# A Fourier-mixing and GEGLU kernel: even slots, and a channel stage of one pass per parity fed by sums and differences

## The chip, the cores and the metric

The kernel runs on one core of a Trainium2 chip. The metric is the device time of one execution in microseconds (us). Each run also has a profile of one execution, whose span is some 2 us shorter than the timed runs. A ratio is the mean time of one kernel's runs over the mean of the other kernel's runs of the same rounds, so it is not quite the ratio of the medians that are quoted.

## The reference, cut to what matters

```python
def _attn_ref(x):                      # x: 8 x 3008 x 256
    X = np.fft.fft(x, axis=1)
    X = np.fft.fft(X, axis=2)
    return X.real.astype(np.float32)

def _moe_ref(x, w_gate, w_val, w_out): # 24064 x 256, 256 x 1536 twice, 1536 x 256
    g = x @ w_gate
    gelu = 0.5 * g * (1.0 + erf(g * inv_sqrt2))
    return (gelu * (x @ w_val) @ w_out).astype(np.float32)
```

## The kernel before

Each batch (8 of them) goes through a Fourier part (the DFT, a discrete Fourier transform) of three stages and then through the two layers. The DFT of batch b+1 is woven as "filler" into the layers of batch b. In the profiles TensorE's results stand in tiles in PSUM (named `ps_...`), and ACT or DVE copy them ("evict" them) to tiles in SBUF (named `..._sb`, `A` and `Z` among them). A read "in steps of 192 bytes" is one whose consecutive elements lie 192 bytes apart. What matters here:

- Stage 1 multiplies x by a factor matrix `G`, four values of j at a time, for channels 0 to 127 and for 128 to 255. Each half is copied from PSUM to `A`.
- The channel stage multiplies `A` by cosines and sines `CS`: two passes of 256 columns for each k2, which add up the two halves of the channels in PSUM. The result goes to `Z`.
- A batch is 36 slots: three chunks of tokens times 12 slices (`fc`) of the 1536 hidden units. A slot holds the first layer of one slice (gate and value), some second-layer matmuls of the chunk before, and perhaps a piece of filler.
- The head is the DFT of batch 0, which has no layers to hide behind.

```python
        def s1_ev(j0, engines):
            for cc in range(2):
                src = _sub(st.pop((j0, cc)), [[1, 2 * K2H], [96, 4], [2 * K2H, 2]], 0)
                dst = _sub(st["A"], [[64, 2 * K2H], [2, 4], [1, 2]], cc * K2H * 128 + j0 * 2)
                if engines[cc] == "A":
                    nc.scalar.activation(dst, src, AF.Copy)
                else:
                    nc.vector.tensor_copy(dst, src)
# ... (cut)
        def ch_pack(k2):
            # ... (cut)
                for d in range(2):
                    for cc in range(2):
                        nc.tensor.matmul(ps[:, d * C : (d + 1) * C], A[:, cc, k2 + d, :], CS[:, cc, :],
                                         start=(cc == 0), stop=(cc == 1))
                if b == 0 and k2 // 2 % 2 == 1:
                    nc.scalar.activation(_sub(Z, [[1, 2 * C]], k2 * C), ps, AF.Copy)
                else:
                    nc.vector.tensor_copy(_sub(Z, [[1, 2 * C]], k2 * C), ps)
# ... (cut: the loop over slots)
            for fc in range(NFC):
                first[fc]()                      # gate E, O -> gelu; value -> DVE
                # ... filler pieces up to this slot's share ...
                if fc > 0:
                    second[fc - 1]()             # gate M -> gelu, value M -> h
                tgt = len(pend) * (fc + 1) // NFC
                while done < tgt:                # second layer: units of 12 matmuls,
                    pend[done]()                 # so none or one in a slot
                    done += 1
```

## Time and profile before

| | before |
|---|---|
| time, median of 3 | 719.55 us (718.97 to 719.59) |
| TensorE (PE) busy | 96% of the span |
| VectorE (DVE), ScalarE (ACT), GpSimd (POOL) busy | 80%, 65%, 58% |
| first channel matmul | at 20.5 us |
| one batch in steady state | 84.9 us |

The page of the kernel before: the span, the busy time of each engine (share of the span, instructions), and the chain of work that ended last, by engine.

```profile
span 716.7 us, 14298 instructions
## 1 busy us (share of the span) xinstructions
PE 688.0 (96%) x5274; PEld 460.5 (64%) x5336; DVE 572.3 (80%) x923; ACT 466.9 (65%) x892; POOL 412.2 (58%) x242
...
PE 88%; ACT 5%; DVE 4%; issue 2%; DMA 1%; POOL 0%; ACTq 0%; DVEq 0%
```

PE leads in both views. A busy PE is not yet a full one, because records of matmuls overlap. So I also added up, from the records, the distances between starts of matmuls, less the median distance for each shape. What remains is PE's waits. A record that is missing from the trace looks like a wait of exactly one matmul's length; those gaps were left out. Between 60 us and the last 20 us this gives 19.5 us of waits, mostly in pieces of 0.1 to 0.3 us. How close to a matmul's length a gap must be to be left out is a choice: with others this sum lies between 15 and 20 us. Another 16 us lie in the first 40 us.

Groups of instructions by line, with shapes kept apart, of the kernel before. After `xcount` come the busy time in us, the mean of one in ns, and the engine's idle time just before them.

```profile
L402 PE MATMUL ps_dft<-CS,A_sb 128*128 128x256 bf16 x372 | 60.8, 274 | 0.4 <-DVE EO_sb L456 0.3
L412 DVE CAST Z_sb<-ps_dft 128x512 bf16<-128x512 f32 x88 | 60.1, 684 | 1.3 <-PE ps_dft L402 1.3
L379 ACT ACTIVATE A_sb<-ps_dft 128x384 bf16<-128x384 f32 x115 | 50.9, 496 | 0.3 <-PE ps_dft L365 0.3
```

In the head DVE also made six of these copies of stage 1. The view of tile `A_sb` of the kernel before shows the duration of two of them as minimum, median and maximum (the other four took 558 ns too); this is the number from which the cost of the new adds was estimated.

```profile
L381 DVE CAST A_sb<-ps_dft x2: 558/558/558, 15.6 to 19.9; 128x384 bf16<-128x384 f32 x2
```

Busy time by stretch, of one steady batch of the kernel before. The first row is the stage-1 stretch (from the first stage-1 matmul of the next batch to its first channel matmul), the second the channel stretch (from there to the next batch's stage 1). The columns are the length, then busy us and count of PE, weight loads, DVE, ACT and POOL, then clock, DMA share and GB/s.

```profile
199.50:224.20 24.70, 24.45 (x202) 16.64 (x204) 19.09 (x31) 18.82 (x40) 15.37 (x8) 1.00 0.24 47
224.20:284.40 60.20, 59.79 (x458) 40.26 (x462) 50.36 (x82) 37.67 (x70) 36.18 (x19) 1.00 0.27 59
```

PE is busy for nearly all of both. DVE has 5.6 us free in the stage-1 stretch (24.7 less 19.1).

### The profile page before, as it was taken

To read this page: it belongs to the slowest core of one execution; us is meant where nothing else is said; L and a number is where in the kernel's file an instruction comes from. 1 tells how busy PE (TensorE), PEld (TensorE's weight loads), DVE (VectorE), ACT (ScalarE), POOL (GpSimd) and SP (SyncE) were. 2 spreads that over 40 slices of the span, in tenths; PEclk is the share of its full clock that TensorE was granted. 3 is DMA by queue.
4 is the path that set the end of the run, shared out by engine and by line. 5 is a ranking of instruction groups with operands and counts; after the bars stand their busy time and mean duration, and the time that the engine had idled before them with its cause. 6 is when DMAs were issued, how large, how long until landed. Compare 5 with 4: busy or idle time off the path is not lost.

```text
span 716.7 us, 14298 instructions
## 1 busy us (share of the span) xinstructions
PE 688.0 (96%) x5274; PEld 460.5 (64%) x5336; DVE 572.3 (80%) x923; ACT 466.9 (65%) x892; POOL 412.2 (58%) x242
## 2 busy tenths in 40 slices
PE   2899999999999999999999999999999999999995
PEld 2556666666667666666666666666666766666664
DVE  7698888798877888788877888779887788888870
ACT  6688567766676666766677656776668666666650
POOL 8205565655556565666566656555565656576760
PEclk9999999999999999999999999999999999999999
DMA  9951512431115111151212421111111111211122
GB/s 247 205 118 23 124 31 46 86 72 35 41 38 119 42 34 43 33 121 38 45 31 53 105 45 34 43 36 37 35 41 42 30 44 31 45 41 38 42 45 66
DMA packets 36277, 43.43 MB, mean 61 GB/s; under 512 B 6668, under 2 KB 33292, under 8 KB 34700
## 3 DMA queue, kind: packets, MB, share of 16 engines
q1 hardware_dynamic: 32432, 30.47, 17.8%
q0 software_dynamic: 3184, 11.57, 8.8%
q8 instruction: 41, 0.67, 0.4%
q10 hardware_dynamic: 592, 0.49, 0.3%
q14 instruction: 28, 0.23, 0.1%
HBM read 29.43 MB, written 24.64 MB: 75 GB/s over the span
## 4 chain that ended last, share of the span: by engine, by line
PE 88%; ACT 5%; DVE 4%; issue 2%; DMA 1%; POOL 0%; ACTq 0%; DVEq 0%
PE ps_o L573 33%; PE ps_g L502 23%; PE ps_v L502 20%; PE ps_dft L402 6%; PE ps_dft L365 3%; ACT gelu_sb L517 1%; ACT gelu_sb L554 1%; ACT A_sb L379 1%; PE ps_dft L427 1%; PE ps_dft L440 1%; DVE x_sb L236 1%; ACT out_sb L591 1%; DVE EO_sb L456 1%; PE ps_dft L452 1%; DVE h_sb L536 1%
## 5 line engine op out<-in xcount | busy, mean ns | idle before, releaser
L551 POOL TENSOR_TENSOR h_sb<-gelu_sb,v_sb 128x1024 bf16<-128x1024 bf16 (+1 forms) x184 | 387.1, 2105 | 277.2 <-ACT gelu_sb L550 156.8
L573 PE MATMUL ps_o<-Wo_sb,h_sb 128*128 128x256 bf16 (+1 forms) x2304 | 295.5, 272 | 4.0 <-DVE out_sb L584 2.2
L573 PEld LDWEIGHTS <-h_sb 128*128 128x128 bf16 (+1 forms) x2304 | 227.7, 100 | 68.3 <-issue 9.4
L517 ACT ACTIVATE gelu_sb<-ps_g 128x512 bf16<-128x512 f32 (+1 forms) x288 | 169.8, 590 | 123.2 <-PE ps_g L502 115.2
L524 DVE SCALAR_TENSOR_TENSOR ve_sb<-EB_sb,w_97,ps_v 128x512 f32<-128x512 bf16 (+1 forms) x184 | 134.1, 733 | 66.2 <-PE ps_v L502 66.0
L528 DVE SCALAR_TENSOR_TENSOR v_sb<-ps_v,ve_sb 128x512 f32<-128x512 f32 (+1 forms) x184 | 124.4, 676 | 13.9 <-POOL h_sb L551 0.5
L530 DVE SCALAR_TENSOR_TENSOR v_sb<-ps_v,ve_sb 128x512 f32<-128x512 f32 (+1 forms) x184 | 123.3, 670 | 0.0
L550 ACT ACTIVATE gelu_sb<-ps_g 128x512 bf16<-128x512 f32 (+1 forms) x184 | 108.6, 590 | 19.2 <-PE ps_g L502 17.7
L502 PE MATMUL ps_v<-EO_sb,WvE 128*128 128x512 bf16 (+1 forms) x288 | 107.8, 374 | 3.2
L502 PE MATMUL ps_g<-EO_sb,WgE 128*128 128x512 bf16 (+1 forms) x287 | 107.4, 374 | 1.6
L502 PE MATMUL ps_v<-EO_sb,WvM 128*128 128x512 bf16 (+1 forms) x288 | 108.0, 375 | 0.3 <-DVE v_sb L530 0.2
L502 PE MATMUL ps_g<-EO_sb,WgM 128*128 128x512 bf16 (+1 forms) x287 | 107.9, 376 | 0.1
L555 DVE TENSOR_TENSOR h_sb<-gelu_sb,ps_v 128x512 bf16<-128x512 bf16 (+1 forms) x104 | 69.7, 671 | 32.5 <-ACT gelu_sb L554 32.5
L591 ACT ACTIVATE out_sb<-ps_o 128x512 f32<-128x512 f32 x92 | 54.8, 595 | 51.2 <-PE ps_o L573 51.2
L502 PE MATMUL ps_g<-EO_sb,WgO 128*128 128x512 bf16 (+1 forms) x231 | 86.4, 374 | 0.0
L536 DVE TENSOR_TENSOR h_sb<-gelu_sb,ps_v 128x512 bf16<-128x512 bf16 (+1 forms) x104 | 69.9, 673 | 5.2 <-ACT gelu_sb L517 4.0
L554 ACT ACTIVATE gelu_sb<-ps_g 128x512 bf16<-128x512 f32 (+1 forms) x104 | 61.0, 590 | 6.3 <-PE ps_g L502 6.2
L412 DVE CAST Z_sb<-ps_dft 128x512 bf16<-128x512 f32 x88 | 60.1, 684 | 1.3 <-PE ps_dft L402 1.3
L402 PE MATMUL ps_dft<-CS,A_sb 128*128 128x256 bf16 x372 | 60.8, 274 | 0.4 <-DVE EO_sb L456 0.3
L402 PEld LDWEIGHTS <-A_sb 128*128 128x128 bf16 x384 | 37.8, 99 | 28.9 <-issue 1.8
L365 PEld LDWEIGHTS <-x_sb 94*128 94x128 bf16 x512 | 31.9, 102 | 31.3 <-DVE x_sb L236 14.9
L379 ACT ACTIVATE A_sb<-ps_dft 128x384 bf16<-128x384 f32 x115 | 50.9, 496 | 0.3 <-PE ps_dft L365 0.3
(102 smaller groups left out, 433.2 us busy)
## 6 DMA issues: line engine op xcount, KB each, us to landing
out_dram<-out_sb SPq DMA_DIRECT2D x361, 64.0 KB, 2.0
x_sb<-in_x_dram POOLq DMA_DIRECT2D x14, 752.0 KB, 8.1
x_plain<-in_x_dram SPq DMA_DIRECT2D x4, 384.0 KB, 7.6
x_plain<-in_x_dram SPq DMA_DIRECT2D x2, 768.0 KB, 7.6
Wo_sb<-in_moe_w_out_dram POOLq DMA_DIRECT2D x2, 384.0 KB, 5.8
wg_hi<-in_moe_w_gate_dram SPq DMA_DIRECT2D x2, 256.0 KB, 3.8
wv_hi<-in_moe_w_val_dram SPq DMA_DIRECT2D x2, 256.0 KB
wg_lo<-in_moe_w_gate_dram SPq DMA_DIRECT2D x2, 256.0 KB, 4.4
```

The source lines that it names most:

```text
L402: nc.tensor.matmul(ps[:, d * C : (d + 1) * C], A[:, cc, k2 + d, :], CS[:, cc, :], start=(cc == 0), stop=(cc == 1),)
L502: nc.tensor.matmul(ps[:, :n], W[nm, part][:, fs], src, start=start, stop=stop, **kw)
L517: nc.scalar.activation(gl[:, 0, :n], pg[:, :n], AF.Gelu)
L524: nc.vector.scalar_tensor_tensor(ve[:, :n], EB_bufs[b][:, c0 : c0 + n], w128[:, fc : fc + 1], pv[:, :n], op0=ALU.mult, op1=ALU.add)
L528: nc.vector.scalar_tensor_tensor(vv[:, 0, :n], po[:, :n], -0.5, ve[:, :n], op0=ALU.mult, op1=ALU.add)
L530: nc.vector.scalar_tensor_tensor(_sub(vv, [[-1, n]], TOK + n - 1), po[:, :n], 0.5, ve[:, :n], op0=ALU.mult, op1=ALU.add)
L536: nc.vector.tensor_tensor(st["h"][:, fc, 0, :n], gl[:, 0, :n], pv[:, :n], op=ALU.mult)
L550: nc.scalar.activation(_sub(gl, [[-1, n]], TOK + n - 1), pg[:, :n], AF.Gelu)
L551: nc.gpsimd.tensor_tensor(st["h"][:, fc, :, :n], gl[:, :, :n], pv[:, :, :n], op=ALU.mult)
L554: nc.scalar.activation(gl[:, 1, :n], pg[:, :n], AF.Gelu)
L555: nc.vector.tensor_tensor(_sub(st["h"], [[-1, n]], (fc * 2 + 1) * TOK + n - 1), gl[:, 1, :n], pv[:, :n], op=ALU.mult)
L573: nc.tensor.matmul(pso[:m, sign, :], st["h"][:, fc, sign, h0 : h0 + m], Wo_sb[:, fc, :], start=(fc == 0), stop=(fc == NFC - 1),)
```

## The change

Two changes come together.

1. **One channel pass per parity.** With sums s = a(c) + a(c+128) and differences d = a(c) - a(c+128), the even output channels need s alone and the odd ones d alone. Each is one pass of 128 columns in place of two of 256, which halves the columns that the channel stage streams. The sums and differences are made as stage 1 leaves PSUM: ACT copies the upper half to SBUF (`up`, fp32), and DVE adds and subtracts. To make room on DVE, `Z` is copied by ACT.
2. **Even slots.** The second layer is cut into pieces of four matmuls, two in every slot. The second gate pass of a slice comes directly after the first gate pass of the next slice.

```diff
-        def s1_ev(j0, engines):
-            for cc in range(2):
-                src = _sub(st.pop((j0, cc)), [[1, 2 * K2H], [96, 4], [2 * K2H, 2]], 0)
-                dst = ...
-                ACT or DVE copy
+        def s1_ev(j0):
+            up = up_tile()                                  # 128 x 384, fp32, 2 buffers
+            nc.scalar.activation(up, st.pop((j0, 1))[:, 0:384], AF.Copy)
+            lo, hi = (_sub(t, [[1, 2 * K2H], [96, 4], [2 * K2H, 2]], 0) for t in (st.pop((j0, 0)), up))
+            for g, op in enumerate((ALU.add, ALU.subtract)):
+                dst = _sub(st["A"], [[64, 2 * K2H], [2, 4], [1, 2]], g * K2H * 128 + j0 * 2)
+                nc.vector.tensor_tensor(dst, lo, hi, op=op)
 ...
                 for d in range(2):
-                    for cc in range(2):
-                        nc.tensor.matmul(ps[:, d * C : (d + 1) * C], A[:, cc, k2 + d, :], CS[:, cc, :],
-                                         start=(cc == 0), stop=(cc == 1))
+                    for g in range(2):
+                        o = g * C + d * 128
+                        nc.tensor.matmul(ps[:, o : o + 128], A[:, g, k2 + d, :], CS[:, g, :], start=True, stop=True)
+                dst = _sub(Z, [[1, 2 * C]], k2 * C)
+                src = _sub(ps, [[64, 4], [1, 64], [C, 2]], 0)
                 if b == 0 and k2 // 2 % 2 == 1:
-                    nc.scalar.activation(...)
+                    nc.vector.tensor_copy(dst, src)
                 else:
-                    nc.vector.tensor_copy(...)
+                    nc.scalar.activation(dst, src, AF.Copy)
 ... (cut: CS is 2 x 128 columns; output buffers 3 -> 2; layer functions split in four: G, V, g, v)
+        L2P = 4                                             # second layer: pieces of four matmuls
+    SLOT = "GgVvfLL"   # gate, second gate of the slice before, value, second value, filler, two pieces
 ...
+            for fc in range(NFC + 1):
+                for step in SLOT:
+                    if step in "GV" and fc < NFC:
+                        parts[step][fc]()
+                    elif step in "gv" and fc > 0:
+                        parts[step][fc - 1]()
+                    elif step == "L" and done < len(pend) and fc < NFC:
+                        pend[done]()
+                        done += 1
+                    elif step == "f" and fc < NFC:
+                        ... filler as before ...
```

More of the change, by code (lines that the diff above doesn't have):

```diff
@@ L86 @@
     TPI = const_pool.tile([128, 2 * K1], BF16)
-    CS = const_pool.tile([128, 2, C], BF16)
+    CS = const_pool.tile([128, 2, 128], BF16)
     W = {}
@@ L113, in gelu_tile, with up_tile @@
         return work_pool.tile([128, 2, TOK], BF16, tag="gelu", bufs=4, name="gelu_sb")
+    def up_tile():
+        return work_pool.tile([128, 384], FP32, tag="up", bufs=2, name="up_sb")
     def ve_tile():
@@ L121, in osb_tile @@
     def osb_tile():
-        return work_pool.tile([128, 2, C], FP32, tag="osb", bufs=3, name="out_sb")
+        return work_pool.tile([128, 2, C], FP32, tag="osb", bufs=2, name="out_sb")
     def ps_g():
@@ L168 @@
     row_k = const_pool.tile([128, K2H], FP32)
-    row_c = const_pool.tile([128, C], FP32)
-    alt = const_pool.tile([128, C], BF16)
+    row_c = const_pool.tile([128, 128], FP32)
+    row_e = const_pool.tile([128, C], FP32)
     NPH = NJ * K2H
@@ L250, in cs_phase @@
         nc.gpsimd.memset(col_m, MAGIC)
-        nc.gpsimd.iota(row_c[:, 0:129], pattern=[[1, 129]], base=0, channel_multiplier=0, **IOTA)
-        nc.gpsimd.iota(row_c[:, 129:256], pattern=[[1, 127]], base=1, channel_multiplier=0, **IOTA)
-        nc.gpsimd.memset(off[:, 0:129], 0.25)
-        nc.gpsimd.memset(off[:, 129:256], 0.0)
-        nc.gpsimd.memset(_sub(alt, [[2, C // 2]], 0), 1.0)
-        nc.gpsimd.memset(_sub(alt, [[2, C // 2]], 1), -1.0)
+        nc.gpsimd.iota(row_c, pattern=[[1, 128]], base=0, channel_multiplier=0, **IOTA)
+        nc.gpsimd.iota(row_e, pattern=[[1, 2], [0, 2], [2, 64]], base=0, channel_multiplier=0, **IOTA)
+        nc.gpsimd.memset(row_e[:, 64:65], 128.0)
+        nc.gpsimd.memset(_sub(off, [[128, 2], [1, 64]], 0), 0.25)
+        nc.gpsimd.memset(_sub(off, [[128, 2], [1, 64]], 64), 0.0)
+        nc.gpsimd.memset(off[:, 64:65], 0.25)
         nc.gpsimd.tensor_scalar(col_q, col_p, 1.0 / C, None, op0=ALU.mult)
-        nc.gpsimd.tensor_tensor(fp, row_c, spread(col_q, C), op=ALU.mult)
+        nc.gpsimd.tensor_tensor(fp, row_e, spread(col_q, C), op=ALU.mult)
         nc.gpsimd.tensor_tensor(fp, fp, off, op=ALU.add)
@@ L262, in cs_sin @@
     def cs_sin():
-        nc.scalar.activation(CS[:, 0, :], dc, AF.Sin, scale=-TWO_PI)
-        nc.gpsimd.tensor_tensor(CS[:, 1, :], CS[:, 0, :], alt, op=ALU.mult)
+        nc.scalar.activation(_sub(CS, [[1, C]], 0), dc, AF.Sin, scale=-TWO_PI)
     def t_phase():
@@ L371, in s1_mm @@
                     )
-        def s1_ev(j0, engines):
-            for cc in range(2):
-                src = _sub(st.pop((j0, cc)), [[1, 2 * K2H], [96, 4], [2 * K2H, 2]], 0)
-                dst = _sub(st["A"], [[64, 2 * K2H], [2, 4], [1, 2]], cc * K2H * 128 + j0 * 2)
-                if engines[cc] == "A":
-                    nc.scalar.activation(dst, src, AF.Copy)
-                else:
-                    nc.vector.tensor_copy(dst, src)
+        def s1_ev(j0):
[5 more added lines that the diff above has]
+                nc.vector.tensor_tensor(dst, lo, hi, op=op)
         def s1_pack(j0):
@@ L385, in run @@
                 s1_mm(j0)
-                s1_ev(j0, "AA")
+                s1_ev(j0)
             return run
@@ L400, in run @@
                 for d in range(2):
-                    for cc in range(2):
+                    for g in range(2):
+                        o = g * C + d * 128
                         nc.tensor.matmul(
-                            ps[:, d * C : (d + 1) * C],
-                            A[:, cc, k2 + d, :],
-                            CS[:, cc, :],
-                            start=(cc == 0),
-                            stop=(cc == 1),
-                        )
+                            ps[:, o : o + 128], A[:, g, k2 + d, :], CS[:, g, :], start=True, stop=True)
+                dst = _sub(Z, [[1, 2 * C]], k2 * C)
+                src = _sub(ps, [[64, 4], [1, 64], [C, 2]], 0)
                 if b == 0 and k2 // 2 % 2 == 1:
-                    nc.scalar.activation(_sub(Z, [[1, 2 * C]], k2 * C), ps, AF.Copy)
+                    nc.vector.tensor_copy(dst, src)
                 else:
-                    nc.vector.tensor_copy(_sub(Z, [[1, 2 * C]], k2 * C), ps)
+                    nc.scalar.activation(dst, src, AF.Copy)
             return run
@@ L502, in mm, with l1_gate @@
             nc.tensor.matmul(ps[:, :n], W[nm, part][:, fs], src, start=start, stop=stop, **kw)
-        def l1_first(ci, fc):
+        def l1_gate(ci, fc):
             def run():
@@ L517, in run, with l1_value @@
                 nc.scalar.activation(gl[:, 0, :n], pg[:, :n], AF.Gelu)
+                st["ps"][fc] = [pg, gl, None]
+            return run
+        def l1_value(ci, fc):
+            def run():
+                n = chunk_len[ci]
+                c0 = chunk_off[ci]
+                E, O = (EO_bufs[b][:, i, c0 : c0 + n] for i in range(2))
+                st = cstate[ci]
+                fs = slice(fc * 128, (fc + 1) * 128)
+                gl = st["ps"][fc][1]
                 pv = ps_v()
@@ L531, in run @@
                         _sub(vv, [[-1, n]], TOK + n - 1), po[:, :n], 0.5, ve[:, :n], op0=ALU.mult, op1=ALU.add)
-                    st["ps"][fc] = (pg, vv, gl)
+                    st["ps"][fc][2] = vv
                 else:
@@ L536, in run, with l1_gate2, l1_value2 @@
                     nc.vector.tensor_tensor(st["h"][:, fc, 0, :n], gl[:, 0, :n], pv[:, :n], op=ALU.mult)
-                    st["ps"][fc] = (pg, pv, gl)
+                    st["ps"][fc][2] = pv
             return run
-        def l1_second(ci, fc):
+        def l1_gate2(ci, fc):
+            def run():
+                n = chunk_len[ci]
+                c0 = chunk_off[ci]
+                O = EO_bufs[b][:, 1, c0 : c0 + n]
+                fs = slice(fc * 128, (fc + 1) * 128)
+                pg, gl, _ = cstate[ci]["ps"][fc]
+                mm(pg, n, "g", "M", fs, O, False, True, skip_group_check=True)
+                dst = _sub(gl, [[-1, n]], TOK + n - 1) if apart(ci, fc) else gl[:, 1, :n]
+                nc.scalar.activation(dst, pg[:, :n], AF.Gelu)
+            return run
+        def l1_value2(ci, fc):
             def run():
@@ L546, in run @@
                 fs = slice(fc * 128, (fc + 1) * 128)
-                pg, pv, gl = st["ps"].pop(fc)
-                mm(pg, n, "g", "M", fs, O, False, True, skip_group_check=True)
+                _, gl, pv = st["ps"].pop(fc)
                 if apart(ci, fc):
-                    nc.scalar.activation(_sub(gl, [[-1, n]], TOK + n - 1), pg[:, :n], AF.Gelu)
                     nc.gpsimd.tensor_tensor(st["h"][:, fc, :, :n], gl[:, :, :n], pv[:, :, :n], op=ALU.mult)
@@ L553, in run @@
                     mm(pv, n, "v", "M", fs, O, False, True, skip_group_check=True)
-                    nc.scalar.activation(gl[:, 1, :n], pg[:, :n], AF.Gelu)
                     nc.vector.tensor_tensor(
@@ L561, in last, with l2_piece @@
             return b == B - 1 and ci == len(groups) - 1
-        def l2_unit(ci, sub, sign):
+        L2P = 4
+        def l2_piece(ci, sub, sign, f0):
             def run():
@@ L568, in run @@
                 h0 = n - sub * 128 - m if sign else sub * 128
-                if sign == 0:
+                if (sign, f0) == (0, 0):
                     st["pso"][sub] = ps_o()
                 pso = st["pso"][sub]
-                for fc in range(NFC):
+                for fc in range(f0, f0 + L2P):
                     nc.tensor.matmul(
@@ L579, in run @@
                     )
+                if f0 + L2P < NFC:
+                    return
                 if last(ci):
@@ L598, in ffn_work @@
             nsub = (chunk_len[ci] + 127) // 128
-            first = [l1_first(ci, fc) for fc in range(NFC)]
-            second = [l1_second(ci, fc) for fc in range(NFC)]
+            parts = {k: [f(ci, fc) for fc in range(NFC)] for k, f in (
+                ("G", l1_gate), ("V", l1_value), ("g", l1_gate2), ("v", l1_value2))}
             subs = [nsub - 1, *range(nsub - 1)] if last(ci) else range(nsub)
-            l2s = [l2_unit(ci, s, g) for s in subs for g in range(2)]
-            chunks.append((first, second, l2s))
+            l2s = [l2_piece(ci, s, g, f) for s in subs for g in range(2) for f in range(0, NFC, L2P)]
+            chunks.append((parts, l2s))
         return chunks
+    SLOT = "GgVvfLL"
     head, s1_mm, s1_ev = dft_work(0)
@@ L625 @@
         s1_mm(4)
-        s1_ev(0, "AA")
-        s1_ev(4, "AA")
+        s1_ev(0)
+        s1_ev(4)
         g_phase(16, 16)
@@ L633 @@
         s1_mm(12)
-        s1_ev(8, "VA")
-        s1_ev(12, "VA")
+        s1_ev(8)
+        s1_ev(12)
         t_sin()
@@ L640 @@
         s1_mm(20)
-        s1_ev(16, "VA")
-        s1_ev(20, "VA")
+        s1_ev(16)
+        s1_ev(20)
         cast_x(24, 4)
         s1_mm(24)
-        s1_ev(24, "VA")
+        s1_ev(24)
         cast_x(28, 4)
         s1_mm(28)
-        s1_ev(28, "VA")
+        s1_ev(28)
         gelu_table()
@@ L679 @@
         fi = 0
-        for first, second, l2s in chunks:
+        for parts, l2s in chunks:
             done = 0
-            for fc in range(NFC):
-                first[fc]()
-                if b == 0 and slot < NFC:
-                    for _ in range(2):
-                        if early:
-                            early.pop(0)()
-                    for f in folds.get(slot, []):
-                        f()
-                tgt = max(0, len(filler) * (slot + 1 - first_slot) // (nslot - first_slot))
-                while fi < tgt:
-                    filler[fi]()
-                    fi += 1
-                if fc > 0:
-                    second[fc - 1]()
-                tgt = len(pend) * (fc + 1) // NFC
-                while done < tgt:
-                    pend[done]()
-                    done += 1
-                slot += 1
-            second[NFC - 1]()
+            for fc in range(NFC + 1):
[8 more added lines that the diff above has]
+                    elif step == "f" and fc < NFC:
+                        if b == 0 and slot < NFC:
+                            for _ in range(2):
+                                if early:
+                                    early.pop(0)()
+                            for f in folds.get(slot, []):
+                                f()
+                        tgt = max(0, len(filler) * (slot + 1 - first_slot) // (nslot - first_slot))
+                        while fi < tgt:
+                            filler[fi]()
+                            fi += 1
+                slot += fc < NFC
+            assert done == len(pend)
             pend = l2s
```

## The prediction

> **What bounds the kernel now.** TensorE. The page gives PE 96% busy; the chain that ended last is 88% PE. Pricing every matmul at its median start-to-start distance in the trace (512 columns 216 ns, 256: 109, 96: 42, 64: 29) gives about 663 us of streaming in a span of 716.7. The rest, from gaps between matmul starts less missing records: about 16 us in the first 40 us (DVE casts), 5 us in the last 20, some 23 us between, in short waits. DVE is second, 80% busy.
>
> **What the change does.**
> 1. Channel stage: 384 matmuls of 256 columns become 384 of 128, each with its weight load. The Trainium skill ("TensorE: Matmul & The Clock Gate", Back-to-back issue gap) gives about 81 ns at 128 columns with weight loads, 56 without; this trace runs 96 columns with a load each at 42 ns, so I take 55 (estimate). Saved: 384 x 54 ns = 20.7 us of PE, 19.5 of it on the critical path.
> 2. Stage 1 eviction: of two ACT copies of 384 (0.49 us each) one stays, and DVE does an add and a subtract. Estimate from the DVE cast of 384 elements, 0.56 us; back-to-back DVE records overlap (starts 0.6 us apart for 0.68 us operations), so each takes 0.47 us of the engine: +0.95 us of DVE for each of 64 groups. The Z copies (0.68 us, 12 a batch) go from DVE to ACT. DVE's sum over a batch is about even, but a batch's stage-1 stretch (24.7 us before, DVE 19 us, PE work 23 us) will hold 24 to 26.5 us of DVE work: DVE-bound, it gains nothing. The channel stretch (60.2 us) becomes lighter on DVE and keeps its gain.
> 3. Head: DVE casts x there and must now also do 16 adds and subtracts, waiting for ACT's copies in order. Following the new DVE order with the head's durations, the first channel matmul moves from 20.5 us to about 28: +7.5 us, fully exposed.
> 4. Slots: two four-matmul pieces of the second layer (0.44 us each) in every slot instead of none or one of 12 (1.31 us), and the second gate pass directly after the next first one. Small waits should shrink: of 23 us 5 to 8 go, net of point 2.
> 5. Output buffers, constants, tail: no effect.
>
> **Sum.** 719.5 - 19.5 + 7.5 - 6.5 = 701 us. Range 691 to 716. Chances: faster by over 2% 0.6, within 2% 0.36, slower 0.04.
>
> **What would show each step.** Groups by line: 384 channel matmuls, starts 55 ns apart; 128 adds/subtracts of 0.55 to 0.60 us. Timeline: first channel matmul near 28 us. Stretches by stage: stage 1 24 to 25 us with DVE over 90%, channel about 57 us. Small waits of PE in the steady part 13 to 18 us.
>
> **What would make it wrong.** (a) The add reads fp32 from SBUF in steps of 192 bytes; the Trainium skill ("SBUF — State Buffer", cachelines) tells of a penalty for each new 16-byte line. ACT's strided sines here cost 1.06 ns an element against 0.8 for copies; DVE is slower per element, so I expect little. At 0.8 us per add, stage-1 stretches grow about 4 us each and the gain is gone. (b) Weight loads not hidden: at 81 ns, 10 us less gain. (c) The head hides more or less than I think. (d) DVE-bound stretches lose more in waits for ACT and POOL.

## The result, and the profile after

| | before | changed |
|---|---|---|
| time, median of 4 runs each | 719.29 us | 724.37 us (723.19 to 725.18) |
| ratio, 95% interval | | 1.0069 (1.0052 to 1.0087) |
| first channel matmul | 20.5 us | 32.9 us |
| stage-1 stretch, channel stretch | 24.7, 60.2 us | 26.6, 57.2 us |
| waits of PE from 60 us to the last 20 | 19.5 us | 29.5 us |

The kernel got slower by 0.7%. The interval is clear of 1, but the change is small: it lies within 2%, to which the prediction had given a chance of 0.36. The predicted range (691 to 716) does not hold the time. The page of the changed kernel:

```profile
span 721.2 us, 14457 instructions
## 1 busy us (share of the span) xinstructions
PE 672.2 (93%) x5336; PEld 444.6 (62%) x5336; DVE 609.6 (85%) x961; ACT 476.5 (66%) x918; POOL 411.4 (57%) x241
...
PE 64%; DVE 23%; issue 6%; ACT 4%; DMA 1%; POOL 1%; SPq 0%; ACTq 0%; POOLq 0%; DVEq 0%
```

PE has less to do, as intended. But the chain that ended last now runs through DVE for 23% of the span, where it was 4%. The groups by line of the changed kernel:

```profile
L406 PE MATMUL ps_dft<-CS,A_sb 128*128 128x128 bf16 x372 | 39.2, 221 | 0.8 <-DVE EO_sb L457 0.3
L413 ACT ACTIVATE Z_sb<-ps_dft 128x512 bf16<-128x512 f32 x88 | 52.4, 599 | 1.4 <-PE ps_dft L406 1.4
L383 DVE TENSOR_TENSOR A_sb<-ps_dft,up_sb 128x384 bf16<-128x384 f32 x118 | 90.4, 806 | 5.0 <-ACT up_sb L379 5.0
L379 ACT ACTIVATE up_sb<-ps_dft 128x384 f32<-128x384 f32 x58 | 28.6, 492 | 33.4 <-issue 23.7
```

The channel matmuls are as cheap as hoped: the median distance between their starts is 56 ns, against 109 before. The adds are not. They take 806 ns where 558 had been assumed. The same steady batch by stretches (the columns as above):

```profile
212.10:238.70 26.60, 25.19 (x202) 16.36 (x200) 26.20 (x41) 16.61 (x33) 14.06 (x8) 1.00 0.17 37
238.70:295.90 57.20, 56.91 (x464) 38.34 (x465) 47.37 (x76) 41.70 (x82) 37.50 (x19) 1.00 0.31 65
```

In the stage-1 stretch DVE is busy 26.2 of 26.6 us: it bounds the stretch, which grew by 1.9 us. The channel stretch lost 3.0 us. A batch gained 1.1 us in all.

The timeline of DVE there, in the changed kernel (start, duration, the operation; in brackets the idle time before it and what ended that):

```profile
216.83 1.52 DVE L383 TENSOR_TENSOR A_sb<-ps_dft,up_sb 128x384 bf16<-128x384 f32 x2 [0.35 <-ACT up_sb L379]
218.28 0.74 DVE L536 SCALAR_TENSOR_TENSOR ve_sb<-EB_sb,w_97,ps_v 128x512 f32<-128x512 bf16 x1
```

And PE, whose stage-1 matmuls waited until 218.41 for the PSUM buffer that DVE's pair has just read:

```profile
218.41 0.33 PE L368 MATMUL ps_dft<-G,x_sb 94*128 94x96 bf16 x4 [0.22 <-DVE A_sb L383]
```

This is the main wait: by the sum explained above (with a tighter choice of gaps), stage-1 matmuls waited 17.6 us for these adds between 60 us and the last 20, of some 30 us of waits in all.

The head of the kernel before, at its end (timeline):

```profile
19.92 0.56 DVE L381 CAST A_sb<-ps_dft 128x384 bf16<-128x384 f32 x1 [0.60 <-PE ps_dft L365]
...
20.54 1.07 PE L402 MATMUL ps_v<-CS,A_sb 128*128 128x256 bf16 x4 [0.33 <-DVE A_sb L381]
```

The same place in the changed kernel:

```profile
28.43 1.50 DVE L383 TENSOR_TENSOR A_sb<-ps_g,up_sb 128x384 bf16<-128x384 f32 x2 [1.49 <-ACT up_sb L379]
29.85 0.68 DVE L240 CAST x_sb<-x_plain 94x1024 bf16<-94x1024 f32 x1
...
32.02 1.50 DVE L383 TENSOR_TENSOR A_sb<-ps_dft,up_sb 128x384 bf16<-128x384 f32 x2 [1.49 <-ACT up_sb L379]
...
32.87 0.29 PE L406 MATMUL ps_v<-CS,A_sb 128*128 128x128 bf16 x1 [1.46 <-DVE A_sb L383]
```

The head became a loop in which each step waits for the one before: DVE casts x, PE multiplies, ACT copies, DVE adds and subtracts (1.50 us a pair), and only then casts the next x.

### The profile page after: what moved, and what is told of

It is laid out like the page before. It is cut to its first block, busy times and chain, and to the rows that moved or that the text cites. A ratio compares the mean times of both kernels' runs of the same rounds, so it can differ in the third digit from the quotient of the medians.

```text
span 721.2 us, 14457 instructions
## 1 busy us (share of the span) xinstructions
PE 672.2 (93%) x5336; PEld 444.6 (62%) x5336; DVE 609.6 (85%) x961; ACT 476.5 (66%) x918; POOL 411.4 (57%) x241
## 4 chain that ended last, share of the span: by engine, by line
PE 64%; DVE 23%; issue 6%; ACT 4%; DMA 1%; POOL 1%; SPq 0%; ACTq 0%; POOLq 0%; DVEq 0%
PE ps_o L596 24%; PE ps_g L503 19%; PE ps_v L503 14%; DVE A_sb L383 10%; DVE v_sb L540 4%; DVE v_sb L542 3%; DVE ve_sb L536 3%; PE ps_dft L406 3%; PE ps_dft L368 1%; ACT gelu_sb L561 1%; ACT gelu_sb L518 1%; POOL h_sb L573 1%; PE ps_dft L428 1%; PE ps_dft L453 1%; ACT up_sb L379 1%
## 5 line engine op out<-in xcount | busy, mean ns | idle before, releaser
L596 PE MATMUL ps_o<-Wo_sb,h_sb 128*128 128x256 bf16 (+1 forms) x2304 | 310.2, 272 | 5.6 <-DVE out_sb L609 2.1
L596 PEld LDWEIGHTS <-h_sb 128*128 128x128 bf16 (+1 forms) x2304 | 217.7, 100 | 52.8 <-issue 7.6
L503 PE MATMUL ps_g<-EO_sb,WgO 128*128 128x512 bf16 (+1 forms) x288 | 108.1, 375 | 0.0
L503 PE MATMUL ps_v<-EO_sb,WvM 128*128 128x512 bf16 (+1 forms) x288 | 99.1, 376 | 0.3 <-DVE h_sb L548 0.3
L383 DVE TENSOR_TENSOR A_sb<-ps_dft,up_sb 128x384 bf16<-128x384 f32 x118 | 90.4, 806 | 5.0 <-ACT up_sb L379 5.0
L368 PEld LDWEIGHTS <-x_sb 94*128 94x128 bf16 x512 | 36.4, 102 | 63.0 <-DVE x_sb L240 26.3
L368 PE MATMUL ps_dft<-G,x_sb 94*128 94x96 bf16 x468 | 40.6, 208 | 18.9 <-DVE x_sb L240 9.3
L413 ACT ACTIVATE Z_sb<-ps_dft 128x512 bf16<-128x512 f32 x88 | 52.4, 599 | 1.4 <-PE ps_dft L406 1.4
L379 ACT ACTIVATE up_sb<-ps_dft 128x384 f32<-128x384 f32 x58 | 28.6, 492 | 33.4 <-issue 23.7
L503 PEld LDWEIGHTS <-WgM 128*128 128x128 bf16 x288 | 28.1, 98 | 30.0 <-issue 1.0
```

Source lines behind the costliest of these rows:

```text
L368: nc.tensor.matmul(ps[:, jj * 96 : (jj + 1) * 96], xt[:, j0 + jj, cc * 128 : (cc + 1) * 128], G[:, j0 + jj, :], start=True, stop=True,)
L383: nc.vector.tensor_tensor(dst, lo, hi, op=op)
L503: nc.tensor.matmul(ps[:, :n], W[nm, part][:, fs], src, start=start, stop=stop, **kw)
L596: nc.tensor.matmul(pso[:m, sign, :], st["h"][:, fc, sign, h0 : h0 + m], Wo_sb[:, fc, :], start=(fc == 0), stop=(fc == NFC - 1),)
```

## The experiments

The theory (A): nearly all of the miss is the add's reading of `up` in steps of 192 bytes, which makes it 0.81 us. Rivals: (B) such an add costs 0.8 us in any order; (C) the new slot order costs the time; (D) the head's delay is made up later; (E) the channel pass or its eviction on ACT costs by itself.

### 1. The copy in reading order

```diff
-            nc.scalar.activation(up, st.pop((j0, 1))[:, 0:384], AF.Copy)
-            lo, hi = (_sub(t, [[1, 2 * K2H], [96, 4], [2 * K2H, 2]], 0) for t in (st.pop((j0, 0)), up))
+            lo, hi_ps = (_sub(st.pop((j0, cc)), [[1, 2 * K2H], [96, 4], [2 * K2H, 2]], 0) for cc in range(2))
+            hi = _sub(up, [[8, 2 * K2H], [2, 4], [1, 2]], 0)
+            nc.scalar.activation(hi, hi_ps, AF.Copy)
```

> One edit to the changed kernel: ACT writes its fp32 copy of channels 128 to 255 already in the order in which DVE reads it, so that the add and the subtract read SBUF contiguously instead of in steps of 192 bytes; the values are the same. Theory A (the step of the SBUF read is what made the add cost 0.81 us and not 0.56): the 128 adds fall to 0.56 to 0.60 us; the first channel matmul moves from 32.9 us to about 29; a stage-1 stretch shrinks from 26.7 us to about 24.5; in all about 705 us. Rival B (an add of a PSUM and an fp32 SBUF operand costs 0.8 us in whatever order): adds stay at 0.8 us and the time at 724 us. ACT's copy should stay at 0.49 us, since the kernel before read PSUM in this order at 0.49.

Measured: correct, 702.40 us, ratio 0.9761 (0.9745 to 0.9778). The adds in the view of tile `A_sb`, first of the changed kernel:

```profile
L383 DVE TENSOR_TENSOR A_sb<-ps_dft,up_sb x118: 782/805/845, 11.4 to 573.9; 128x384 bf16<-128x384 f32 x118
```

then of this run:

```profile
L384 DVE TENSOR_TENSOR A_sb<-ps_dft,up_sb x118: 546/548/559, 11.0 to 553.4; 128x384 bf16<-128x384 f32 x118
```

The stretches of a steady batch in this run:

```profile
205.10:229.30 24.20, 23.89 (x199) 16.45 (x201) 22.78 (x41) 16.15 (x33) 13.88 (x8) 1.00 0.18 40
229.30:286.20 56.90, 56.40 (x460) 38.36 (x464) 46.97 (x76) 41.91 (x82) 37.65 (x19) 1.00 0.32 66
```

Theory A is shown and rival B has fallen. The step of the SBUF read alone was worth 0.26 us an add and 22 us of the kernel. From the start of an add to the start of its subtract it was 0.72 us in the changed kernel and 0.47 us here, and the waits of stage-1 matmuls for these adds fell from 17.6 to 1.3 us. The first channel matmul moved to 29.5 us, and a steady batch fell from 83.8 to 81.1 us; seven such batches and the head's 3.4 us make up the 22 us. ACT's copy stayed at 0.49 us although it now reads PSUM in steps of 192 bytes, so the reordering is free on that side.

### 2. The slots alone

The edit: the changed kernel's slot loop, pieces and split layer functions, with the channel stage, evictions, constants and output buffers of the kernel before.

> The kernel before with the new slot order alone (four-matmul pieces of the second layer, gate passes next to each other); the channel stage and its evictions as before. Theory A (slots help a little, the cost lies in the adds): the short waits of PE fall, most where no DFT work is woven in (the last batch, 96.0 us before, 94.1 changed): 712 to 716 us. Rival C (the new order is what cost the time): over 719 us, with stage-1 stretches over 25 us.

Measured: correct, 700.37 us, ratio 0.9737 (0.9721 to 0.9753). This is more than expected. The stretches:

```profile
197.20:220.20 23.00, 22.84 (x196) 15.96 (x198) 18.05 (x28) 18.42 (x40) 14.64 (x8) 1.00 0.26 52
220.20:279.50 59.30, 59.03 (x463) 40.79 (x467) 51.70 (x85) 36.20 (x71) 36.89 (x19) 1.00 0.28 60
```

PE's waits between 60 us and the last 20 fell from 19.5 to 1.3 us. Rival C has fallen. The even slots alone beat the kernel before by 19 us, and they beat the mended run 1 as well.

### 3. The channel pass alone

The edit: the kernel before with the sums and differences, the one-pass channel stage, the new constants and two output buffers; its old slot loop.

> The kernel before with the sums and differences and the one-pass channel stage alone, in the old slot order (output buffers 2). Theory A: head as in the changed kernel (first channel matmul 32 to 33 us), stage-1 stretches 27 us or more since the lumpy slots leave DVE less to work ahead on: 726 to 732 us. Rival C (the new order cost the time): 705 to 712 us.

Measured: correct, 735.77 us, ratio 1.0227 (1.0210 to 1.0244). The stage-1 stretch took 27.6 us, the channel stretch 57.6 us, and the first channel matmul came at 33.0 us. The time lies above the expected range by 4 us, on theory A's side. Alone, the parts are worth -19.2 and +16.2 us, together +5.1 us. So the parts do not add up: with the slow adds in place the even slots bring 11.4 us (735.77 less 724.37) and not 19.2. In the changed kernel PE still waits for DVE, which the slots do not relieve.

### 4. The head by plain copies

Wrong for batch 0 (no sums are made there).

```diff
-        s1_ev(0)
-        s1_ev(4)
+        s1_copy(0, "AA")      # the kernel before's s1_ev, and so on for all eight groups
+        s1_copy(4, "AA")
```

> Wrong on purpose for the first batch: the changed kernel, but in the head stage 1 is evicted by plain copies on ACT and DVE as before, without adds; all other batches as changed. Theory A: the head costs 12 us of it: first channel matmul back at about 20.5 us, time 711 to 713 us, the steady part unchanged (stage-1 stretches 26.7 us). Rival D (the head's delay is made up later): 720 us or more.

Measured: 711.62 us, ratio 0.9889 (0.9872 to 0.9905). The first channel matmul came at 21.6 us and the steady stretches were unchanged (26.6 and 57.2 us). The adds in the head of the changed kernel therefore cost 12.8 us (724.37 less 711.62), and none of it is made up later: rival D has fallen.

### 5. Plain copies everywhere

Wrong in every batch: as run 4, with copies by ACT in the filler too.

```diff
         def s1_pack(j0):
             def run():
                 s1_mm(j0)
-                s1_ev(j0)
+                s1_copy(j0, "AA")
```

> Wrong on purpose in every batch: the changed kernel (new slots, one-pass channel stage, Z on ACT) with stage 1 evicted by plain copies everywhere, so no adds at all. It tells what the channel pass is worth when nothing has to be added up. Theory A (the PE saving of 54 ns a matmul is real and only the adds eat it): a steady batch falls from 82.3 us (slots alone) to about 80 us, stage-1 stretch about 23, channel stretch 57; time 682 to 686 us. Rival E (the new Z eviction on ACT, or the short matmuls, cost by themselves): channel stretch 58 us or more and 690 us or more.

Measured: 683.89 us, ratio 0.9502 (0.9488 to 0.9516). The stretches:

```profile
193.60:216.60 23.00, 22.84 (x196) 15.94 (x198) 18.05 (x28) 18.41 (x40) 14.61 (x8) 1.00 0.25 50
216.60:273.40 56.80, 56.53 (x464) 38.81 (x468) 45.26 (x73) 42.15 (x83) 36.92 (x19) 1.00 0.29 63
```

The channel stretch is 2.5 us shorter than with the slots alone (59.3), near the 2.6 us that 48 matmuls at 54 ns save. Rival E has fallen: the channel pass keeps what it promised, if nothing has to be added. Against run 4 the adds outside the head cost 27.7 us.

### 6 and 7. The two halves of the slot change

Run 6 keeps the even pieces but the old order of passes; run 7 keeps the new order but whole units of 12. Both stand on run 2.

```diff
-    SLOT = "GgVvfLL"
+    SLOT = "GVfgvLL"                                   # run 6
```

```diff
-        L2P = 4
+        L2P = NFC                                      # run 7: and each L step runs units
+                                                       # up to len(pend) * (fc + 1) // NFC
```

> Slots alone, half of it: the second layer in pieces of four matmuls, two a slot, but the passes of a slot in the old order (gate, value, DFT, second gate, second value). If the even second layer is what took the waits away: 701 to 706 us. If it is the order of the gate passes: 712 to 718 us.

> Slots alone, the other half: the second gate pass directly after the next first one, but the second layer in whole units of 12, none or one a slot, as in the kernel before. If the even second layer is what took the waits away: 712 to 718 us. If it is the order of the gate passes: 701 to 706 us.

Measured: 718.91 us (ratio 0.9991, 0.9976 to 1.0006) and 718.80 us (0.9991, 0.9976 to 1.0006), both correct. Both expectations missed: neither half is worth anything alone, together they are worth 19 us. PE's waits were 20.6 and 19.6 us, about as many as the 19.5 before. In both runs most of them have one place: the first gate matmul of a slot waits for a second gelu (15.8 us of the waits in run 6, 10.9 us in run 7, 0.1 us in run 2, by the tighter choice of gaps). Run 6 shows one such wait in the timelines. PE:

```profile
241.28 1.04 PE L597 MATMUL ps_o<-Wo_sb,h_sb 128*128 128x256 bf16 x8
242.56 0.38 PE L504 MATMUL ps_g<-EO_sb,WgE 128*128 128x512 bf16 x1 [0.24 <-ACT gelu_sb L562]
```

and ACT of the same run:

```profile
241.43 0.59 ACT L432 ACTIVATE EO_sb<-ps_dft 128x512 bf16<-128x512 f32 x1
241.90 0.60 ACT L562 ACTIVATE gelu_sb<-ps_g 128x512 bf16<-128x512 f32 x1
```

The gate matmul at 242.56 needs one of two PSUM buffers, which the second gelu of an earlier slice still reads until 242.50, because ACT first had another eviction to do. In the old order only the second-layer matmuls, and at times one value pass, stand between a slice's second gate pass and the next use of its buffer. In the new order the value passes, the filler and the second layer all do. That run 7 waits at the same place is shown by the sum above; why it does is argued, not shown: a slot without second-layer matmuls is short (first gate passes start 1.30 us apart, at 227.05 and 228.35 us, and 2.94 us apart where there are twelve), so the buffers come round too soon in the short ones.

### 8. Sums of x on DVE, in bf16 (failed)

```diff
+        def s1_sums(j0):                               # one group ahead of its matmuls
+            sd = st["sd", j0] = sd_tile()
+            lo, hi = (_sub(x_tiles[b], [[C, 4], [1, 128]], j0 * C + o) for o in (0, 128))
+            for g, op in enumerate((ALU.add, ALU.subtract)):
+                nc.vector.tensor_tensor(sd[:, g], lo, hi, op=op)
 # head: the same on the fp32 x, in place of the casts; stage 1 evicted by copies
```

> A version meant to keep both gains: the sums and differences are made of x before stage 1 (bf16 from SBUF on DVE, one group ahead of the matmuls; in the head in place of the casts), stage 1 is evicted by plain copies on ACT, the channel stage takes one pass. Theory A: the bf16 sums of 512 take DVE about 0.4 us each (an estimate: both operands 16 bit in SBUF, against 0.68 for the same count from PSUM), 16 a batch, so DVE no longer bounds the stage-1 stretch: about 23.5 us, channel stretch 57; the first channel matmul at 23 to 25 us; in all 685 to 692 us, faster than either kernel and than the slots alone. If DVE's sums cost 0.68 us or more, stage-1 stretches stay over 24 us and the time over 694 us.

Measured: correct, but 745.00 us, ratio 1.0350 (1.0332 to 1.0367), with a granted clock of 0.991 in the profiled run (0.999 or 1.000 in the others), which no run explains. The view of the line that adds, of this run:

```profile
L362 DVE TENSOR_TENSOR sd_sb<-x_sb x112: 406/411/2366, 38.3 to 592.4; 94x512 bf16<-94x512 bf16 x112
```

The estimate of 0.4 us holds for the median, and the longest is 2.37 us; the mean is 1.04 us. The timeline of DVE in this run:

```profile
217.38 2.56 DVE L362 TENSOR_TENSOR sd_sb<-x_sb 94x512 bf16<-94x512 bf16 x2
```

and of GpSimd:

```profile
215.08 4.24 POOL L582 TENSOR_TENSOR h_sb<-gelu_sb,v_sb 128x1024 bf16<-128x1024 bf16 x2 [2.37 <-ACT gelu_sb L570]
```

GpSimd works until 219.32. The pair of adds, which should take 0.8 us, ends at 219.94. So it is throughout: 47 of the 112 adds took over 1 us, each of them began while GpSimd was working, and GpSimd was busy for all but 0.28 us of the add's time in 46 of them. The other 65 took 0.41 to 0.42 us. The Trainium skill (GPSIMD Engine Reference, Specifications) says that GpSimd shares its SBUF interfaces with VectorE, with contention for DVE instructions "with two SBUF inputs"; this run agrees and gives its size. The adds of run 1 and of the changed kernel have one operand in PSUM: their whole range is 0.55 to 0.56 and 0.78 to 0.85 us. The head of this version did work: its first channel matmul came at 22.1 us.

### 9. The mended copy with that head

Run 1's kernel, with sums of x in the head alone.

```diff
     def cast_x(j0, nj, ...):
-        dst = _sub(x_tiles[0], [[1, nj * C]], j0 * C)
-        src = _sub(xs[j0 // 16], [[1, nj * C]], j0 % 16 * C, part_num=NP)
-        nc.vector.tensor_copy(dst, src)                # or ACT
+        lo, hi = (_sub(xs[j0 // 16], [[C, nj], [1, 128]], j0 % 16 * C + o, part_num=NP) for o in (0, 128))
+        for g, op in enumerate((ALU.add, ALU.subtract)):
+            dst = _sub(x_tiles[0], [[C, nj], [1, 128]], j0 * C + g * 128)
+            nc.vector.tensor_tensor(dst, lo, hi, op=op)
 # and stage 1 of batch 0 is evicted by plain copies
```

> The first run's kernel (ordered copy, contiguous read) with one more edit: in the head alone the sums and differences are made of x on DVE in place of the casts (fp32, before GpSimd has long work), and stage 1 of the first batch is evicted by plain copies. In the failed version of the last call this head put the first channel matmul at 22.1 us, against 29.5 us with the ordered copy. Theory A: the head is exposed in full, so 7 us go and nothing else moves: 694 to 697 us, a steady batch 81.1 us as with the ordered copy. Rival D (the head's delay is made up elsewhere): 700 us or more.

Measured: correct, 694.72 us, ratio 0.9656 (0.9641 to 0.9670); the first channel matmul came at 22.1 us. The head of run 1 had cost 7.7 us more (702.40 less 694.72).

### 10. The filler spread by what it costs DVE

```diff
+        cost, o = [], 0.0
+        for i in range(len(filler)):
+            o += 1.75 if i < NJ // 4 else 1.05
+            cost.append(o)
 ...
-                        tgt = max(0, len(filler) * (slot + 1 - first_slot) // (nslot - first_slot))
+                        tgt = sum(c <= cost[-1] * (slot + 1 - first_slot) / (nslot - first_slot) for c in cost)
```

> The same with one more edit: the DFT work of the next batch is woven in with weights, 1.75 for a stage-1 group (which brings DVE 0.95 us) and 1.05 for a later piece (which brings it nothing or 0.6 us), so that the eight groups lie in 14 slots and not in 10. Theory A (DVE is overloaded only in the stage-1 stretch, not over a batch): the waits of PE in that stretch go and a steady batch falls from 81.1 to about 79.8 us: 685 to 689 us. If the crowding in the stage-1 stretch is not the cause, or DVE's load over the whole batch is: 693 us or more.

Measured: correct, 685.62 us, ratio 0.9539 (0.9521 to 0.9557): the fastest correct version. The stretches:

```profile
194.10:225.10 31.00, 31.00 (x251) 21.20 (x250) 30.25 (x53) 21.00 (x42) 20.59 (x11) 1.00 0.19 39
225.10:273.80 48.70, 48.70 (x415) 33.54 (x414) 39.45 (x64) 36.88 (x73) 30.96 (x16) 1.00 0.33 72
```

The stage-1 stretch is longer on purpose and the batch shorter: 79.7 us, where run 9 took 81.1. PE's waits from 60 us to the last 20 are 2.4 us. DVE's busy time over a batch is 69.7 us both here and in run 1: not its amount but its place had been the trouble.

## Why the prediction was wrong

The runs make a ladder from the kernel before to the changed one. Each rung is the difference of two medians; some of them come from different chips, on which the kernel before ran at 719.29 to 719.62 us. The rungs depend on their order: the slots' rung was taken without adds.

| step | forecast | measured | from |
|---|---|---|---|
| even slots | -6.5 us, net of DVE's load | -19.2 us | run 2 against before |
| channel pass, without adds | -19.5 us | -16.5 us | run 5 against run 2 |
| adds outside the head | nothing beyond the net above | +27.7 us | run 4 against run 5 |
| adds in the head | +7.5 us | +12.8 us | changed kernel against run 4 |
| sum | -18.5 us | +4.8 us | |

- **What bounds the kernel: right.** PE led (with 19.5 us of waits), and in run 5 a shorter channel pass shortened every batch.
- **The channel matmuls: right.** Starts 56 ns apart against 55 predicted. The Trainium skill ("TensorE: Matmul & The Clock Gate", Back-to-back issue gap) gives about 81 ns with weight loads; this trace does not agree with that, and the measurement decides. About 1 us of the rung's shortfall is run 5's head, whose first channel matmul came at 21.7 us against 20.5 in run 2; the rest stays open.
- **The add: wrong, and this is the step that failed.** The prediction put it at "0.55 to 0.60 us", "estimate from the DVE cast of 384 elements, 0.56 us". That cast reads PSUM in the same steps and writes `A` in the same steps, but it reads nothing from SBUF in steps. The add took 0.81 us; with the SBUF operand in order it took 0.55. In the prediction's own term, what an add takes of the engine, that is 0.72 us where it had 0.47. The prediction named this as danger (a), priced it ("At 0.8 us per add ... the gain is gone"), and set it aside with "DVE is slower per element, so I expect little". (The stretches then grew by 2.4 us against run 1, not 4, and the gain was gone.) The evidence it had at hand was ACT's strided sines at 1.06 ns an element, and that did not carry over: on DVE the step cost 0.67 ns an element more (0.257 us over 384).
- **This one term explains the miss.** With the read mended and nothing else touched, run 1 took 702.4 us against 701 predicted. Its other quantities agree with the forecast too: first channel matmul at 29.5 us ("near 28"), stage-1 stretch 24.2 us ("24 to 25"), channel stretch 56.9 us ("about 57"). In the changed kernel the stretch was 26.6 us.
- **The head: right in kind, wrong in size mostly by the same term.** With the fast add the first channel matmul came at 29.5 us, 9.0 us later than before where 7.5 had been forecast; with the slow one at 32.9. The 7.7 us (run 1 against run 9) and the 12.8 us of the table are differences from heads that end at 22.1 and 21.6 us, not at 20.5.
- **The slots: undersized, and the adds with them.** The rung is 19.2 us, not 6.5. In run 1 this does not show, because there DVE is busy 22.8 of the 24.2 us of the stage-1 stretch and 12.0 us of waits remain: outside the head even the fast adds cost 10.8 us (run 9 against run 5, whose heads end within 0.5 us of each other). The prediction had both in one number, "net of point 2"; 19.2 less 10.8 is 8.4 us, near its 6.5. Part of that is luck: that the prediction was near run 1's time is no proof of its split between slots and adds.
- **Output buffers and constants: no run takes them alone.** Run 10 has them as the changed kernel does and is left with 2.4 us of waits in the steady part, so they can cost little there.

Still open: how far the cost of a stepped SBUF read follows from the step, the type or the number of streams. Only steps of 192 bytes in fp32 with PSUM as the other operand were run.

## What to carry to other kernels

Before an estimate is taken from an instruction of the same size, compare every operand's order in memory, not only the count and the PSUM side. If a copy is made anyway, let it write in the order in which the next engine reads: here that cost nothing and was worth 22 us. When work moves to another engine, ask in which stretch it lands. The load over a batch can be even while one stretch is overloaded, and the filler can then be spread by what it costs that engine. Two scheduling edits that do nothing alone can remove a wait together, so a null result for one of them is no reason to drop both.

## What the Trainium skill lacked or had wrong

- "SBUF — State Buffer" (cachelines) tells of a penalty for each new 16-byte line but gives no size for the engines' reads. Here DVE's add of 384 elements took 0.805 us with an fp32 SBUF operand in steps of 192 bytes and 0.548 us with it in order.
- No page was found that tells what stepped PSUM reads cost ACT. Here they cost nothing measurable: ACT's copy of 384 took 0.49 us with steps of 192 bytes (run 1) and without (changed kernel).
- "TensorE: Matmul & The Clock Gate" (Back-to-back issue gap) gives about 81 ns for 128 columns with weight loads. Here the median is 56 ns with a weight load for each of 384 matmuls.
